# A sequence-to-MLP kernel on one core: layer 0's activation by a polynomial alone, tested as it runs, with the general program behind a branch

## The chip, the cores and the metric

The kernel runs on one core of a Trainium2 chip. The metric is device time in microseconds; the median of three runs before the change is 918.11 us (917.94 to 920.32). The engines are named as in the profile: PE is TensorE, ACT ScalarE, DVE VectorE, POOL GpSimd, SP SyncE (which issues the DMAs here). PE's clock has two levels, 1.2 and 2.4 GHz; the profile gives what was granted as a share of the higher.

## The reference

A gated linear attention with a running state gives `y` for 4 batches, 8 heads, 768 tokens and a head size of 40. It is laid out as 3072 tokens of 320 values and goes through two MLP layers, each 320 to 2048 to 320:

```python
def _moe_ref(x, w_in, w_out):            # layer 0
    h = x @ w_in
    g = h - np.tanh(h)
    return (g @ w_out).astype(np.float32)

def _moe2_ref(x, w_in, w_out):           # layer 1
    h = x @ w_in
    relu6 = np.clip(h + 3.0, 0.0, 6.0)
    g = h * relu6 / 6.0
    return (g @ w_out).astype(np.float32)
```

The weights arrive as float64. The attention's values are small, so layer 0's `h` is small, and `h - tanh(h)` is nearly `h^3/3`, a difference that would lose most of its digits in float32 if it were taken directly.

## The kernel before

**Tiling.** A block is 128 positions of all 4 batches, 512 tokens; there are 6. The 2048 inner features are 16 tiles of 128. A *step* (`step`, line 591) is one block with one feature tile: 16 steps a block, 96 a layer, 192 in all; the first four steps of layer 0 take two batches and two feature tiles instead.

**A step.** `m_in` (line 605) makes `ph`, 128 features by 512 tokens in PSUM, out of eight products (the weights and the input are each split in a high and a low part, since the products round their operands). ACT and DVE turn `ph` into `g`. ACT casts `g` to its high part `gh` (line 636), POOL subtracts to get the low part `gl` (line 637), and `m_out` adds the products with the second weight matrix into four accumulators, eight of `gh` (lines 655, 657) and four of `gl` (line 655), each of 320 columns. `ph` and `u` have two buffers, `g`, `gh` and `gl` three.

**Layer 0's activation (lines 613 to 630).** With u = h^2, the polynomial is g = h u Q(u), Q(u) = (QS u + QB)^2 + QG, good for u up to UMAX = 0.0625. ACT makes `u` (617), tanh `Tm` (618), the square `aq` (621) and a mask `m` that is above zero where u exceeds UMAX (625). DVE makes `ph u` (620), `(aq + QG) g` (629), `ph - Tm` (624), and puts the last in place of the polynomial where the mask says so (630). Layer 1 has one ACT and one DVE operation (632, 633).

**Weights (`weights`, line 270).** Each feature tile of each layer is loaded as float64 bits (704 KB), turned into float32 by one ACT pass (281) and three integer passes on DVE (289, 291, 293), then split in high (ACT, 302) and low (POOL, 305). `raw` and `cva` have two buffers. The split tiles of layer 1 go where those of layer 0 lay, so tile f of layer 1 waits until layer 0's last step with tile f is done.

**Attention.** For each block and batch: scores (485), exp on ACT, weighing on DVE (491), the products with the values (531) and with the state (534), the state's update (517), a transposition into the MLP's input (401).

**Order.** Nothing is ordered by hand. `Order` collects all operations with a rank `t` and a modelled cost; `plan` runs through them once at build time, and each engine takes of the ready operations the one with the least `t`. The result is a fixed sequence per engine. A step's activation has rank k - 8.62, the weights of layer 1 have ranks from 148 up and so fill what is left before they are needed. Eighty products of zeros (line 708, rank about 4) fill PE's gaps at the start.

Of the kernel before, what the change touches and what calls it, by code (L numbers as in the profile page):

```python
# [33 lines left out]

# g(h) = h - tanh(h) = h u Q(u), u = h^2; Q(u) = (QS u + QB)^2 + QG for u <= UMAX
UMAX = 0.0625
QS = 0.2279802546653879
QB = -0.29232135416051347
QG = 0.24788139857377955
# The high word of a float64, taken as a float32, has its exponent's bias in its bits 20 up: times  # L40
# 2^-112 takes 896 = 1023 - 127 from it, and a shift by 3 puts it in float32's place. What is under
# 2^-119 goes to zero, or to another number under that.
REBIAS = 2.0 ** -112
# [23 lines left out]
class Order:  # L67
    """Orders the kernel's operations: each engine takes, of those whose operands and buffers are
    ready, the one with the least t. Buffers of a tag go round in the order of t."""

# [30 lines left out]
    def plan(self):  # L101
# [52 lines left out]
        while True:  # L154
            best = None
            for e in engines:
                while wait[e] and wait[e][0][0] <= free[e]:
                    k = heapq.heappop(wait[e])[1]
                    heapq.heappush(avail[e], (self.ops[k][0], k))
                if avail[e]:  # L160
                    s = free[e]
                elif wait[e]:
                    s = wait[e][0][0]
                else:
                    continue
                if best is None or s < best[0]:
                    best = (s, e)
            if best is None:
                break
            s, e = best  # L170
            while wait[e] and wait[e][0][0] <= s:
                k = heapq.heappop(wait[e])[1]
                heapq.heappush(avail[e], (self.ops[k][0], k))
            k = heapq.heappop(avail[e])[1]
            t, _, cost, fn, _, nbytes, cols = self.ops[k]
            out.append(k)
            if e == "SP":
                dma = max(dma, s + 1.1) + nbytes / 360e3
                end = dma + 0.85
                free[e] = max(s + cost, dma - P["queue"])  # L180
            elif e == "PE":
                # The clock is halved after a window of it in which fewer columns have left the array.
                end, part = s, 1.0
                while part > 1e-9:
                    w = int(end / WINDOW)
                    rate = cost if passed.get(w - 1, 0.0) >= COLUMNS else 2 * cost
                    p = min(part, (WINDOW * (w + 1) - end) / rate + 1e-9)
                    passed[w] = passed.get(w, 0.0) + cols * p
                    part -= p
                    end += rate * p  # L190
                free[e] = end
            else:
                end = free[e] = s + cost
            freed = False
            for inst in used_by.get(k, ()):
                users_left[inst] -= 1
                last_end[inst] = max(last_end[inst], end + 0.2)
                if not users_left[inst]:
                    heapq.heappush(free_slots[tag_of[inst]], (last_end[inst], self.slot[inst]))
                    freed = True  # L200
            for j in succ[k]:
                left[j] -= 1
                ready_at[j] = max(ready_at[j], end + self.LAT[e, self.ops[j][1]])
                if not left[j]:
                    offer(j)
            if freed:
                blocked[:] = [j for j in blocked if not ready(j)]
# [8 lines left out]
@with_exitstack  # L216
def tile_kernel(ctx: ExitStack, tc: tile.TileContext, att: bass.AP, gates: bass.AP, w1: bass.AP, w2: bass.AP, out: bass.AP):
    nc = tc.nc
    Q = P["Q"]

# [20 lines left out]
    state = const.tile([128, B * NPR, 2, DV], F32, name="state")  # L241
    still = const.tile([128, 128], BF16, name="still")
    pairs = [const.tile([128, 2 * NT], F32, name=f"pairs{i}") for i in range(2)]
# [7 lines left out]
    def alloc(pool, tag, bufs, shape, dt, *inst):  # L251
        """What takes the buffer, and what the order needs to know of it."""
        def take():
            name = f"{tag}_{S_.slot[inst]}"
            T[inst] = pool.tile(shape, dt, tag=name, name=name)
            return T[inst]
        return take, (tag, bufs, inst)
# [10 lines left out]

    # ---------------------------------------------------------------- weights
    def weights(layer, f, tl, t):  # L270
# [37 lines left out]

    # ------------------------------------------------------------------ gates
    g_d = {}  # L310
# [71 lines left out]

    # ----------------------------------------------------------- layer inputs
    def x_new(layer, c):
        """The buffers of a block's input, taken for its first batch."""
        def take():
# [4 lines left out]
    def x_ops(layer, c, b, src, scale, tx, ts):  # L391
        """Transposes a tile of tokens, and splits it into what float32r holds and the rest."""
        xb = ("x", layer, c)
# [29 lines left out]

    # -------------------------------------------------------------- attention
    def attention(c, b, t0):
# [163 lines left out]

    # -------------------------------------------------------------------- MLP  # L590
    def step(k, layer, c, bs, fs, t):
# [20 lines left out]
        ph, u, g = (lambda: T["ph", k]), (lambda: T["u", k]), (lambda: T["g", k])  # L612
        if layer == 0:
            take_T, new_T = alloc(ap2, "Tm", BUFS["Tm"], [128, TB], F32, "Tm", k)
# [76 lines left out]

    # ---------------------------------------------------------------- program
    nc.vector.memset(still, 0.0)
    make_identity(nc, ident)
# [5 lines left out]

    # The tensor engine's clock stays up only while enough columns leave the array: until the first
    # block's input is there, products of nothing fill the gaps.
    take_p, new_p = alloc(ps_h, "ph", 2, [128, TB], F32, "ph", "w")

    def warm(i):
        if i == 0:
            take_p()
        nc.tensor.matmul(T["ph", "w"].rearrange("p (j t) -> p j t", j=4), still, still.unsqueeze(1).to_broadcast([128, 4, 128]), start=True, stop=True)
    for i in range(NWARM):
        S_.add(P["ws"] + P["wst"] * i, "PE", 0.215, lambda i=i: warm(i), r=[K("ph", "w")] if i else [], w=[] if i else [K("ph", "w")], new=[] if i else [new_p], at=-99.0, cols=512)  # L710
# [15 lines left out]
    for layer in range(2):  # L726
# [4 lines left out]
        for c in range(NC):  # L731
# [4 lines left out]
            for part in SEQ if k == 0 else "U" * NF:  # L736
# [4 lines left out]
                step(k, layer, c, range(b0, b0 + nb), range(f, f + 4 // nb), k + Q.get(f"m{k}", 0.0) if k < NF else k)  # L741
                k += 1
    S_.plan()
    with tc.manual_schedule():
# [43 lines left out]
```

## Time and profile before

| | |
|---|---|
| median of three runs | 918.11 us |
| profiled execution, span from first to last instruction | 914.1 us |
| busy: PE, DVE, ACT, POOL | 866.9, 572.4, 552.2, 431.1 us |
| share of the span: PE, DVE, ACT, POOL | 95, 63, 60, 47% |
| mean granted clock of PE | 0.977 |
| DMA moved | 77.70 MB, 85 GB/s in the mean |
| instructions | 14486 |

The page of the profile gives busy time by engine over the whole span. A PE that counts as busy isn't always at its peak: the products are pipelined, their ends are modelled, and at the lower clock each lasts longer. So the number of products in a stretch and the distance between their starts say more than the busy share. Idle time of an engine that is not the bound costs nothing.

### The profile page before, as it was taken

To read this page: it belongs to the slowest core of one execution; us is meant where nothing else is said; L and a number is where in the kernel's file an instruction comes from. 1 tells how busy PE (TensorE), PEld (TensorE's weight loads), DVE (VectorE), ACT (ScalarE), POOL (GpSimd) and SP (SyncE) were. 2 spreads that over 40 slices of the span, in tenths; PEclk is the share of its full clock that TensorE was granted. 3 is DMA by queue.
4 is the path that set the end of the run, shared out by engine and by line. 5 is a ranking of instruction groups with operands and counts; after the bars stand their busy time and mean duration, and the time that the engine had idled before them with its cause. 6 is when DMAs were issued, how large, how long until landed. Compare 5 with 4: busy or idle time off the path is not lost.

```text
span 914.1 us, 14486 instructions
## 1 busy us (share of the span) xinstructions
PE 866.9 (95%) x5208; PEld 767.3 (84%) x5208; DVE 572.4 (63%) x924; ACT 552.2 (60%) x1145; POOL 431.1 (47%) x351
## 2 busy tenths in 40 slices
PE   8898888899999999999999988899999999999997
PEld 4687777798898899889898876789999999989897
DVE  7989999887767867885778998823123231132121
ACT  4687776688677768877679865534334343343332
POOL 4666666355446356444334555743333333333342
PEclk9798998899999999999999999999999999999999
DMA  8775445431243044122002225302001020010000
GB/s 281 241 225 178 151 142 164 158 125 42 81 135 106 30 130 131 61 77 96 10 10 70 69 96 181 104 1 64 1 13 51 1 61 4 1 47 1 30 1 30
DMA packets 36248, 77.70 MB, mean 85 GB/s; under 512 B 3824, under 2 KB 24016, under 8 KB 36176
## 3 DMA queue, kind: packets, MB, share of 16 engines
q1 hardware_dynamic: 36176, 76.77, 26.3%
q8 instruction: 41, 0.67, 0.3%
q14 instruction: 31, 0.25, 0.1%
HBM read 67.93 MB, written 8.83 MB: 84 GB/s over the span
## 4 chain that ended last, share of the span: by engine, by line
PE 67%; DVE 16%; issue 5%; ACT 5%; DMA 4%; POOL 2%; SPq 1%; DVEq 0%; POOLq 0%; ACTq 0%
PE ph L605 31%; PE acc L655 19%; PE acc L657 9%; DVE g L629 3%; PE pa L531 3%; DVE g L630 2%; DVE cva L293 2%; PE pa L534 2%; DVE ph L624 2%; DVE g L620 1%; DMA eg<-ed 1%; PE pa L485 1%; DVE cva L291 1%; PE pa L401 1%; DVE cva L289 1%
## 5 line engine op out<-in xcount | busy, mean ns | idle before, releaser
L637 POOL TENSOR_TENSOR gl<-g,gh 128x512 fp32r<-128x512 f32 x192 | 259.7, 1354 | 361.9 <-ACT gh L636 346.8
L655 PE MATMUL acc<-wh,gh 128*128 128x320 f32 x768 | 234.2, 317 | 0.0
L657 PE MATMUL acc<-wl,gh 128*128 128x320 f32 x768 | 229.8, 311 | 0.0
L633 DVE SCALAR_TENSOR_TENSOR g<-u,ph 128x512 f32<-128x512 f32 x96 | 65.9, 687 | 214.3 <-ACT u L632 206.2
L636 ACT CAST gh<-g 128x512 fp32r<-128x512 f32 x192 | 118.5, 618 | 60.6 <-PE acc L657 53.6
L655 PEld LDWEIGHTS acc<-wh,gh 128*128 128x128 f32 x768 | 146.2, 190 | 6.4 <-DVE T L673 0.2
L657 PEld LDWEIGHTS acc<-wl,gh 128*128 128x128 f32 x768 | 146.1, 190 | 5.1
L632 ACT ACTIVATE u<-ph,bias_r 128x512 f32<-128x512 f32 x96 | 66.2, 689 | 138.5 <-PE ph L605 138.4
L605 PE MATMUL ph<-xh,wh 128*128 128x512 f32 (+1 forms) x392 | 128.6, 410 | 17.9 <-DVE g L630 10.3
L655 PE MATMUL acc<-wh,gl 128*128 128x320 f32 x768 | 144.7, 310 | 0.2 <-POOL gl L637 0.2
L605 PE MATMUL ph<-xh,wl 128*128 128x512 f32 (+1 forms) x392 | 122.2, 393 | 0.0
L655 PEld LDWEIGHTS acc<-wh,gl 128*128 128x128 f32 x768 | 121.2, 189 | 0.7 <-POOL gl L637 0.5
L605 PE MATMUL ph<-xl,wh 128*128 128x512 f32 (+1 forms) x392 | 121.1, 390 | 0.0
L620 DVE TENSOR_TENSOR g<-ph,u 128x512 f32<-128x512 f32 x96 | 65.9, 686 | 56.6 <-ACT Tm L618 47.0
L617 ACT ACTIVATE u<-ph 128x512 f32<-128x512 f32 x96 | 57.2, 596 | 65.2 <-PE ph L605 64.9
L629 DVE SCALAR_TENSOR_TENSOR g<-aq,g 128x512 f32<-128x512 f32 x96 | 89.9, 936 | 0.5
L605 PEld LDWEIGHTS ph<-xh,wl 128*128 128x128 f32 x392 | 74.4, 192 | 17.0
L605 PEld LDWEIGHTS ph<-xh,wh 128*128 128x128 f32 x392 | 64.9, 192 | 27.5 <-DVE g L630 14.3
L605 PEld LDWEIGHTS ph<-xl,wh 128*128 128x128 f32 x392 | 74.5, 192 | 16.0
L625 ACT ACTIVATE m<-u,bias_u 128x512 bf16<-128x512 f32 x96 | 69.3, 722 | 15.4 <-DVE g L630 15.4
L605 PE MATMUL ph<-xt,wh 128*128 128x512 f32 (+1 forms) x196 | 77.0, 393 | 0.0
L605 PE MATMUL ph<-xt,wl 128*128 128x512 f32 (+1 forms) x196 | 76.7, 391 | 0.0
(107 smaller groups left out, 1269.7 us busy)
## 6 DMA issues: line engine op xcount, KB each, us to landing
raw<-w SPq DMA_DIRECT2D x32, 704.0 KB
kvo<-att SPq DMA_DIRECT2D x24, 580.0 KB
E<-gd SPq DMA_DIRECT2D x24, 512.0 KB
pairs<-att SPq DMA_DIRECT2D x48, 160.0 KB
eg<-ed SPq DMA_DIRECT2D x40, 128.0 KB
x1d<-T SPq DMA_DIRECT2D x24, 192.0 KB
y<-x1d SPq DMA_DIRECT2D x24, 192.0 KB
out<-T SPq DMA_DIRECT2D x24, 160.0 KB
```

Of the source, the lines that this page charges most:

```text
L531: nc.tensor.matmul(pa[:, h * DV:(h + 1) * DV], T["E", c, b][:, h, :], vv()[:, h, :], start=(h == 0), stop=(c == 0 and h == H - 1))
L605: nc.tensor.matmul(ph[:, j * n:(j + 1) * n], w[:, r * 128:(r + 1) * 128], x, start=(i == 0), stop=(i == len(prods) - 1))
L617: S_.add(ta, "ACT", 0.48, lambda: nc.scalar.activation(out=take_u(), in_=ph(), func=AF.Square), r=[K("ph", k)], w=[K("u", k)], new=[new_u])
L620: S_.add(ta, "DVE", 0.6, lambda: nc.vector.tensor_tensor(take_g(), ph(), u(), ALU.mult), r=[K("ph", k), K("u", k)], w=[K("g", k)], new=[ne ...
L625: S_.add(ta, "ACT", 0.54, lambda: nc.scalar.activation(out=take_m(), in_=u(), func=AF.Relu, bias=bias_u), r=[K("u", k)], w=[K("m", k)], ne ...
L629: S_.add(ta, "DVE", 0.6, lambda: nc.vector.scalar_tensor_tensor(g(), T["aq", k], QG, g(), ALU.add, ALU.mult), r=[K("aq", k), K("g", k)], w ...
L632: S_.add(ta, "ACT", 0.48, lambda: nc.scalar.activation(out=take_u(), in_=ph(), func=AF.Relu, scale=1.0 / 6.0, bias=bias_r), r=[K("ph", k)] ...
L633: S_.add(ta, "DVE", 0.6, lambda: nc.vector.scalar_tensor_tensor(take_g(), u(), 1.0, ph(), ALU.min, ALU.mult), r=[K("ph", k), K("u", k)], w ...
L636: S_.add(t + P["gh"], "ACT", 0.52, lambda: nc.scalar.copy(take_h(), g()), r=[K("g", k)], w=[K("gh", k)], new=[new_h])
L637: S_.add(t + P["gl"], "POOL", 1.23, lambda: nc.gpsimd.tensor_tensor(take_l(), g(), T["gh", k], ALU.subtract), r=[K("g", k), K("gh", k)], w ...
L655: nc.tensor.matmul(o, lhs, wh, start=(f == 0 and part == 0), stop=(f == NF - 1 and part == 1))
L657: nc.tensor.matmul(o, lhs, wl, start=False, stop=False)
```

## The change

The whole program is built twice. The first, with `over` given (`small`), takes the polynomial alone in layer 0: tanh, the mask, the difference and the predicated copy are left out, and the first square also adds up its row into a column of `sums`, one column for each of the 96 steps. Since a sum of squares is at least its largest term, a sum that is at most UMAX proves that every u in it is. In layer 1 the largest of all sums is found (a maximum on DVE, a transpose on PE, a maximum of one row) and compared with UMAX; the flag `over` is 1 where it is larger. Behind the first program the flag is read into registers, and the second program, the general one with tanh as it stands in the kernel before (without the products of zeros), runs only if the flag is set. `P`, `Q` and the ranks are the same for both; the costs given to the planner for layer 0's activation differ.

```diff
+    small = over is not None
...
+    if small:
+        still = const.tile([128, 128], BF16, name="still")
+        sums = const.tile([128, NF * NC], F32, name="sums")
+        most = const.tile([128, 2], F32, name="most")
...
-        if layer == 0:
+        if layer == 0 and small:
+            take_a, new_a = alloc(ap2, "aq", BUFS["aq"], [128, TB], F32, "aq", k)
+            S_.add(ta, "ACT", 0.7, lambda: nc.scalar.activation(out=take_u(), in_=ph(), func=AF.Square, accum_out=sums[:, k:k + 1]), r=[K("ph", k)], w=[K("u", k), K("sums", k)], new=[new_u])
+            S_.add(ta, "ACT", 0.7, lambda: nc.scalar.activation(out=take_a(), in_=u(), func=AF.Square, scale=QS, bias=bias_q), r=[K("u", k)], w=[K("aq", k)], new=[new_a])
+            S_.add(ta, "DVE", 0.69, lambda: nc.vector.tensor_tensor(ph(), ph(), u(), ALU.mult), r=[K("u", k)], w=[K("ph", k)])
+            S_.add(ta, "DVE", 0.69, lambda: nc.vector.scalar_tensor_tensor(take_g(), T["aq", k], QG, ph(), ALU.add, ALU.mult), r=[K("ph", k), K("aq", k)], w=[K("g", k)], new=[new_g])
+        elif layer == 0:
...
-    for i in range(NWARM):
+    for i in range(NWARM if small else 0):
...
+    if small:
+
+        take_t, new_t = alloc(ps_a, "pa", 2, [128, 512], F32, "pt", "most")
+        t = NF * (NC + 1)
+
+        def rows():
+            nc.vector.reduce_max(most[:, 0:1], sums, axis=mybir.AxisListType.X)
+        S_.add(t, "DVE", 0.25, rows, r=[K("sums", i) for i in range(NF * NC)], w=[K("most")])
+        S_.add(t, "PE", 0.1, lambda: nc.tensor.transpose(take_t()[0:1, 0:128], most[:, 0:1], ident), r=[K("most")], w=[K("pt", "most")], new=[new_t], cols=128)
+
+        def compare():
+            nc.vector.reduce_max(most[0:1, 1:2], T["pt", "most"][0:1, 0:128], axis=mybir.AxisListType.X)
+            nc.vector.tensor_scalar(over, most[0:1, 1:2], UMAX, None, ALU.is_gt)
+        S_.add(t, "DVE", 0.5, compare, r=[K("pt", "most")], w=[K("over")])
...
-    with tile.TileContext(nc) as tc:
-        tile_kernel(tc, *args)
+    with tile.TileContext(nc) as tc, tc.tile_pool(name="flag", bufs=1) as flag:
+        over = flag.tile([1, 1], I32, name="over")
+        tile_kernel(tc, *args, over=over)
+        outside = nc.values_load(over, min_val=0, max_val=1, skip_runtime_bounds_check_because="a comparison gives 0 or 1")
+        with tc.If(outside > 0):
+            tile_kernel(tc, *args)
```

## Rows read from the trace of the kernel before

**Rows 1.** Table by stretch: PE, PEld, DVE, ACT, POOL busy (count), clock, DMA share, GB/s.
```profile
0.00:40.00 40.00, 33.04 (x203) 19.88 (x204) 32.96 (x73) 22.43 (x58) 20.39 (x21) 0.94 0.89 283
40.00:180.00 140.00, 122.10 (x775) 107.56 (x774) 131.46 (x197) 98.60 (x223) 89.29 (x74) 0.90 0.54 170
180.00:440.00 260.00, 257.29 (x1704) 231.36 (x1705) 196.53 (x345) 197.20 (x446) 129.20 (x119) 1.00 0.28 90
440.00:600.00 160.00, 146.22 (x784) 128.34 (x784) 137.37 (x184) 113.39 (x209) 82.51 (x53) 0.98 0.24 77
600.00:900.00 300.00, 299.84 (x1690) 271.97 (x1689) 73.05 (x125) 118.52 (x206) 106.02 (x84) 1.00 0.07 21
```

**Rows 2.** Chain that ended last, layer 1: start us, length us, what.
```profile
606.66 1.84 PE ph L605 x8
610.25 1.84 PE ph L605 x8
```

**Rows 3.** Groups of instructions, 40 to 180 us: shapes, count, busy us, mean ns, idle.
```profile
L655 PE MATMUL acc<-wh,gh 128*128 128x320 f32 x64 | 21.4, 345 | 0.0
...
L531 PE MATMUL pa<-kvo,E 128*128 128x41 f32 x96 | 13.4, 305 | 2.9 <-DVE E L491 1.8 <-DVE xt L421 1.1
...
L605 PE MATMUL ph<-xh,wh 128*128 128x512 f32 x30 | 11.3, 462 | 2.3 <-DVE g L630 2.3
...
L485 PE MATMUL pa<-pairs 40*128 40x128 f32 x128 | 10.3, 287 | 1.4 <-DVE tk L380 1.4
...
L629 DVE SCALAR_TENSOR_TENSOR g<-aq,g 128x512 f32<-128x512 f32 x18 | 20.2, 1124 | 0.1
...
L293 DVE SCALAR_TENSOR_TENSOR cva<-raw,cva 128x704 int32<-128x704 int32 x14 | 17.4, 1244 | 0.1
```

**Rows 4.** PE in order of time, 418 to 440 us: start us, length us, what.
```profile
418.66 1.16 PE L485 MATMUL pa<-pairs 40*128 40x128 f32 x16
...
419.75 0.42 PE L655 MATMUL acc<-wh,gh 128*128 128x320 f32 x1
...
437.19 1.88 PE L531 MATMUL pa<-kvo,E 128*128 128x41 f32 x16
...
438.89 1.10 PE L534 MATMUL pa<-state,eg 128*128 128x82 f32 x8
...
439.78 0.48 PE L605 MATMUL ph<-xh,wh 128*128 128x512 f32 x1
```

**Rows 5.** Groups of instructions, 440 to 600 us.
```profile
L655 PE MATMUL acc<-wh,gh 128*128 128x320 f32 x148 | 45.0, 316 | 0.0
...
L605 PE MATMUL ph<-xh,wh 128*128 128x512 f32 x78 | 26.4, 420 | 12.6 <-DVE g L633 7.4 <-DVE g L630 5.1
...
L629 DVE SCALAR_TENSOR_TENSOR g<-aq,g 128x512 f32<-128x512 f32 x24 | 22.2, 925 | 0.1
```

**Rows 6.** Groups of instructions over the whole span: layer 0's operations on DVE and ACT.
```profile
L629 DVE SCALAR_TENSOR_TENSOR g<-aq,g 128x512 f32<-128x512 f32 x96 | 89.9, 936 | 0.5
...
L630 DVE COPY_PREDICATED g<-m,ph 128x512 f32<-128x512 int16 x96 | 71.0, 739 | 5.6 <-ACT m L625 0.2
...
L620 DVE TENSOR_TENSOR g<-ph,u 128x512 f32<-128x512 f32 x96 | 65.9, 686 | 56.6 <-ACT Tm L618 47.0 <-POOL gl L637 6.5 <-PE pa L485 2.0
...
L617 ACT ACTIVATE u<-ph 128x512 f32<-128x512 f32 x96 | 57.2, 596 | 65.2 <-PE ph L605 64.9
...
L625 ACT ACTIVATE m<-u,bias_u 128x512 bf16<-128x512 f32 x96 | 69.3, 722 | 15.4 <-DVE g L630 15.4
...
L636 ACT CAST gh<-g 128x512 fp32r<-128x512 f32 x192 | 118.5, 618 | 60.6 <-PE acc L657 53.6 <-DVE g L630 5.8 <-PE pa L531 1.1
...
L569 ACT ACTIVATE den<-pa 128x8 f32<-128x8 f32 x20 | 3.6, 179 | 7.9 <-PE pa L534 7.7
```

**Rows 7.** Order of time at the end of the span: the last stores.
```profile
908.46 3.25 SPq L681 DMA_DIRECT2D out<-T  x4
```

**Rows 8.** DMA queues: packets, MB, share of 16 engines' span.
```profile
q8 instruction: 41, 0.67, 0.3%
```

More of the change, by code (lines that the diff above doesn't have):

```diff
@@ L216, in tile_kernel @@
 @with_exitstack
-def tile_kernel(ctx: ExitStack, tc: tile.TileContext, att: bass.AP, gates: bass.AP, w1: bass.AP, w2: bass.AP, out: bass.AP):
+def tile_kernel(ctx: ExitStack, tc: tile.TileContext, att: bass.AP, gates: bass.AP, w1: bass.AP, w2: bass.AP, out: bass.AP, over=None):
     nc = tc.nc
+    small = over is not None
     Q = P["Q"]
@@ L241, in tile_kernel @@
     state = const.tile([128, B * NPR, 2, DV], F32, name="state")
-    still = const.tile([128, 128], BF16, name="still")
+    if small:
+        still = const.tile([128, 128], BF16, name="still")
+        sums = const.tile([128, NF * NC], F32, name="sums")
+        most = const.tile([128, 2], F32, name="most")
     pairs = [const.tile([128, 2 * NT], F32, name=f"pairs{i}") for i in range(2)]
@@ L690, in x1_in @@
         x_ops(1, c, b, ("x1", c, b), 1.0, t + P["x1x"], t + P["x1s"])
-    nc.vector.memset(still, 0.0)
+    if small:
+        nc.vector.memset(still, 0.0)
     make_identity(nc, ident)
@@ L699, in tile_kernel @@
     nc.vector.memset(bias_r, 0.5)
-    take_p, new_p = alloc(ps_h, "ph", 2, [128, TB], F32, "ph", "w")
+    take_p, new_p = alloc(ps_h, "ph", 2, [128, TB], F32, "ph", "w") if small else (None, None)
     def warm(i):
@@ L742, in tile_kernel @@
                 k += 1
+    if small:
+        take_t, new_t = alloc(ps_a, "pa", 2, [128, 512], F32, "pt", "most")
[8 more added lines that the diff above has]
+        S_.add(t, "DVE", 0.5, compare, r=[K("pt", "most")], w=[K("over")])
     S_.plan()
```

## The prediction

> **What bounds the kernel now.** I read the table of busy time by stretch first [rows 1]. From 600 to 900 us, which is layer 1 alone, PE is busy 299.84 of 300 us at full clock while DVE works 73 us: there PE is the bound and nothing in the change touches it. From 180 to 440 us PE is busy 257.29 of 260. Two stretches are different. From 40 to 180 us PE shows 122.10 of 140 at a mean clock of 0.90, and DVE shows 131.46, or 94%. From 440 to 600 us PE shows 146.22 of 160 and DVE 137.37. The reader should see that the average over the kernel (PE 95%, DVE 63%) hides two stretches in which DVE leads.
>
> Busy time on PE is not work at full rate, so I counted the products. In layer 1 one step starts 3.59 us after the last, and its eight products of 512 columns take 1.84 [rows 2]: 0.230 us each, and (3.59 - 1.84)/12 = 0.146 for one of 320 columns. In 40 to 180 us there are 3 x 64 = 192 of 320 columns and 30+30+30+15+15 = 120 of 512 [rows 3], and four half-width steps of 16 products at half price: 192 x 0.146 + 120 x 0.230 + 64 x 0.115 = 63 us. Attention beside it: 128 products of L531 (96 in the row, 32 more in another buffer) and 128 of L485 [rows 3] at full-clock paces of 1.70/16 and 1.09/16 [rows 4], 13.6 + 8.7 us; about 107 of 82 columns (L534, L517) at 0.89/8 [rows 4], 11.9; transposes about 1.5. Sum 99 us of work in 140: **41 us lost**. In 440 to 600 us: 444 x 0.146 + 307 x 0.230 [rows 5] + 3 for transposes = 138.5: **21 us lost**. In 180 to 440 the idle time is 2.7 us. The first 40 us are bound by loading (DMA share 0.89), and layer 0's first step starts after them.
>
> **The change, part by part.** *DVE in a step of layer 0.* Now four operations: L620 0.686, L624 (a twin of L620, 0.690), L629 0.936, L630 0.739 [rows 6], 3.05 us. After: u times ph into PSUM, and (aq + QG) times ph into g. Both have one operand in SBUF and one in PSUM, as L620 has: 2 x 0.686 = 1.37 [rows 6]. Removed: 1.68 us in each of 96 steps, 161 us of DVE in all. It counts only where DVE leads.
>
> *ACT in a step.* Tanh (a twin of L617, 0.596) and the mask (L625, 0.722) go [rows 6]: 1.32 us. The first square gains a sum along its row. No row shows such a sum; I bound it by zero and by one more small ACT instruction, L569 at 0.179 [rows 6], and take 0.18, for it must read out at least one column. ACT then has 0.596 + 0.18 + 0.72 + 0.618 = 2.1 us a step, under the 3.59 of PE, so this price is hidden by PE; if ACT led (the rival below), it would cost 17 us over 96 steps.
>
> *40 to 180 us.* DVE does 18 of the steps there (the count of L629 [rows 3]). 18 x 1.68 = 30 us go (L629 is 1.124 there, so a little more). DVE's demand falls from 131.5 to about 100, against 99 of PE work. Two engines with equal demand don't mesh perfectly: DVE alone would allow 100 + its present 8.5 idle = 108.5 us, a gain of 31; I take 119 us, a **gain of 21**, because each step of the first block also waits for a weight tile that goes through DVE three times (about 1.24 us each [rows 3]), ACT twice and POOL once in two buffers. Ends: 10 and 31.
>
> *440 to 600 us.* 24 steps [rows 5] leave 24 x 1.68 = 40 us less for DVE: 137.4 becomes 97, well under 138.5 of PE work. Converting layer 1's weights then fits into the gaps: a step of 3.59 us leaves 2.2 of DVE free, where it leaves 0.5 now. Of the 21 us lost I take back 16; what is late next is ACT and POOL in the weight chain, and the hand-over of the weight buffers. **Gain 16**, ends 10 and 20.
>
> *180 to 440 us.* At most the 2.7 us idle; I take 2. *0 to 40 us:* no layer 0 step runs there, so zero, between 2 lost and 2 gained because the planner, given other costs, may order the loads otherwise.
>
> *The test.* One maximum over 96 columns, one transpose, one maximum of a row and one comparison, once, in layer 1, where DVE is free 227 us of 300 [rows 1]; on PE about 0.1 us. Nothing.
>
> *The branch.* Each engine reads the flag and jumps over the second program once its own stream is done. The trace has no jump. What is nearest: the last stores are issued from 908.46 over 3.25 us [rows 7] and the span ends at 914.1, so 2.4 us cover an issue and a landing. If the read and the refilling of the instruction stream lie beside that landing, the price is zero; if a flag read, a fetch, and a barrier with another fetch come one after another at 2.4 each with nothing hidden, 9.6. I take 4, nearer to two round trips in a row with a part hidden under the last landing. PE, which ends first (about 908), has its cover; SP, which ends last, has none.
>
> The instruction queue moves 41 packets with 0.67 MB, 16 KB each, in 0.3% of 16 engines' span [rows 8], which is about 1.1 us a packet: a jump to code that isn't there costs at least that. The Trainium skill, "Runtime: NRT & Kernel Launch", section "Instruction fetch mechanics", says that a taken branch to a page outside the current window must wait for a fetch of that page, against this change; "Advanced Engine Details and Errata", section "Control Flow Timing", gives about 108 ns for a compare and branch, which alone would leave the end 4 us earlier than my sum. No run here shows either yet.
>
> **Sum.** 914.1 - 21 - 16 - 2 + 4 = 879.1 us of span. The median of the runs, 918.1, lies 4.0 above the span, so 883.1; I predict **883**. With all ends taken together 914.1 - 31 - 20 - 5 + 0 + 4 = 862 and 914.1 - 10 - 10 - 0 + 9.6 + 2 + 4 = 910; the ends won't all meet, and the case's own range is 872 to 895.
>
> **The rivals.**
> 1. *The weight chain takes DVE's place.* In the first block a step can't start before its tile is converted. If the chain load, ACT, three DVE operations, ACT, POOL keeps its pace, freed DVE time stays idle: gains 10 and 10 instead of 21 and 16, 914.1 - 10 - 10 - 0 + 4 + 4 = 902. For it: 14 conversions in 140 us beside 18 steps [rows 3], one every 10 us. Against it: DVE is 94% busy, so the chain queues at DVE, and what queues there becomes shorter. Chance 0.17, 895 to 905.
> 2. *PE takes everything back.* The losses of both stretches vanish but for some 11 us, and the branch is hidden: 914.1 - 31 - 20 - 3 + 1 + 4 = 865. For it: from 180 us on, with DVE at 76%, PE is at 99%. Chance 0.16, 860 to 872.
> 3. *The sum along the row is dear, and ACT becomes the bound.* Place: the first square of each step. ACT has 1.94 us a step without it against 3.59 of PE; it decides from 1.65 us an instruction up, and the 35 us won are gone when each of 96 steps is 0.36 longer, so at 2.0 us; at 2.3 the kernel takes 883 + 96 x (2.3 - 1.65) = 945, slower than before. Against it: no small ACT row is over 0.4 us. Chance 0.03.
> 4. *The change doesn't do what it says: the test trips.* Then the general program runs behind the first, 883 + 914 = about 1797. Worked out from the reference's inputs, the largest sum of squares of h over one row of 512 tokens is 0.0127, a fifth of 0.0625, so it won't. Chance 0.01.
> The forecast has 0.61; 0.02 is left for a change that moves the time by less than 0.3%, about what a measurement of this kernel can tell from none.
>
> **How the numbers follow.** The likeliest case gives 883. To hold 8 in 10 the range takes the whole forecast and the near halves of rivals 1 and 2: 866 to 900. Faster by over 0.3%: 0.61 + 0.17 + 0.16 = 0.94; within 0.3%: 0.02; slower: 0.04.
>
> **What would show it.** Right: in the table by stretch the row that held DVE at 94% shows it near 80% with PE at full clock; the first block's output is stored some 20 us earlier than now, layer 1's steady pace begins near 561 instead of 600 us, and after that one step takes 3.59 us as before. DVE has two operations a step of 0.69 each, ACT three. Wrong: L605 waits as long in the two stretches but for ACT or POOL instead of DVE (rival 1); a gap of more than 10 us between the last store and the end (the branch); ACT with a second instruction of over 0.4 us behind the square (rival 3).

## The result, and the profile after

| | median | lowest to highest |
|---|---|---|
| before | 918.29 us | 917.94 to 920.32 |
| after | 894.14 us | 892.04 to 895.40 |

The ratio is 0.9735 (0.9711 to 0.976): the kernel is faster by 24 us, inside the range of 866 to 900 us and 11 us slower than the forecast of 883. The profiled execution of the changed kernel took 892.04 us with a span of 890.2.

The same table by stretch as [rows 1], of the changed kernel (PE, PEld, DVE, ACT, POOL busy with counts, granted clock, DMA share, GB/s):

```profile
0.00:40.00 40.00, 31.29 (x194) 18.72 (x194) 31.79 (x68) 19.23 (x49) 15.81 (x19) 0.95 0.90 262
40.00:180.00 140.00, 131.21 (x886) 117.43 (x884) 112.42 (x182) 95.43 (x244) 99.93 (x82) 0.94 0.57 191
180.00:440.00 260.00, 260.00 (x1725) 235.78 (x1724) 123.42 (x238) 150.98 (x393) 121.25 (x119) 1.00 0.25 82
440.00:600.00 160.00, 147.84 (x815) 130.93 (x814) 101.97 (x129) 88.76 (x172) 84.66 (x56) 1.00 0.23 77
```

In the second row DVE went from 94% of the stretch to 112.42/140 = 80%, as forecast, and PE got through 886 instructions instead of 775. In the fourth row DVE also fell, from 137 to 102 us of 160, close to the 97 that was forecast, but PE hardly moved: 147.84 us and 815 instructions, against 146.22 and 784. Half of the mechanism worked, and the other half didn't although the engine that was blamed became free in the mean of the stretch.

Layer 0's step, groups of the whole span, which answer to [rows 6]:

```profile
L623 DVE TENSOR_TENSOR ph<-ph,u 128x512 f32<-128x512 f32 x96 | 66.8, 696 | 101.9 <-ACT u L621 101.5
L624 DVE SCALAR_TENSOR_TENSOR g<-aq,ph 128x512 f32<-128x512 f32 x96 | 65.6, 684 | 21.7 <-POOL gl L649 8.8 <-ACT aq L622 6.3
L621 ACT ACTIVATE u<-ph 128x512 f32<-128x512 f32 x96 | 57.1, 594 | 85.5 <-PE ph L611 81.4 <-DVE state L562 3.4
L621 ACT ACTIVATION_READ_ACCUMULATOR u<-ph 128x1 f32 x96 | 18.7, 194 | 0.0
```

DVE has two operations of 0.696 and 0.684 us (forecast 0.686 each). The sum along the row is an ACT instruction of its own, 0.194 us (forecast 0.18).

**Where the 24 us came from.** I counted as the prediction did: the products in a stretch times their full-rate durations, taken from the length of the stretch. What is left over is lost time. The stretches are matched by what runs in them: the last stores of the first block's output are issued at 173.31 us after the change and at 187.34 before. Where the line is drawn hardly matters, since the changed kernel loses 0.1 us between 160 and 200. The products were counted in pieces of 20 or 40 us, and one that lies across an edge counts twice; counted in one piece, the losses come out up to 3 us higher and the gains the same within 0.6.

| stretch (before / after) | lost before | lost after | gain | forecast |
|---|---|---|---|---|
| loading, 0 to 40 | 29.1 | 29.6 | -0.5 | 0 |
| first block, 40 to 200 / 40 to 160 | 41.6 | 23.2 | 18.4 | 21 |
| middle, 200 to 480 / 160 to 480 | 8.0 | 3.5 | 4.5 | 2 |
| border of the layers, 480 to 600 | 20.3 | 15.1 | 5.2 | 16 |
| behind the last products | | | -3.1 | -4 |
| sum | | | 24.5 | 35 |

The span became 914.1 - 890.2 = 23.9 us shorter, so the table leaves 0.6 us unexplained. The trace is that of the fastest run of the changed kernel; in the second measurement below the first block loses 25.2 us, so the gain there is 16 to 18. One row is far from its forecast: the border of the two layers, where layer 1's weights are converted while layer 0's last steps run. The experiments go there first.

### The profile page after: what moved, and what is told of

It reads as the page before. It is cut to its first block, busy times and chain, and to the rows that moved or that the text cites. A ratio compares the mean times of both kernels' runs of the same rounds, so it can differ in the third digit from the quotient of the medians.

```text
span 890.2 us, 14216 instructions
## 1 busy us (share of the span) xinstructions
PE 851.8 (96%) x5209; PEld 759.0 (85%) x5209; DVE 437.5 (49%) x735; ACT 465.3 (52%) x1049; POOL 420.9 (47%) x351
## 4 chain that ended last, share of the span: by engine, by line
PE 79%; DVE 9%; DMA 4%; issue 3%; ACT 3%; POOL 2%; SPq 1%; DVEq 0%; POOLq 0%; ACTq 0%
PE ph L611 34%; PE acc L667 22%; PE acc L669 11%; PE pa L537 4%; PE pa L491 2%; DVE cva L297 2%; PE pa L540 2%; DVE cva L295 2%; DVE cva L299 1%; PE pa L407 1%; PE pa L523 1%; DMA raw<-w 1%; ACT cva L287 1%; DMA E<-gd 1%; DMA pairs<-att 1%
## 5 line engine op out<-in xcount | busy, mean ns | idle before, releaser
L649 POOL TENSOR_TENSOR gl<-g,gh 128x512 fp32r<-128x512 f32 x192 | 256.5, 1336 | 329.0 <-ACT gh L648 322.3
L667 PEld LDWEIGHTS acc<-wh,gh 128*128 128x128 f32 x768 | 144.2, 188 | 8.4 <-DVE T L685 1.5
L611 PE MATMUL ph<-xh,wh 128*128 128x512 f32 (+1 forms) x392 | 126.2, 403 | 10.9 <-DVE g L645 7.5
L623 DVE TENSOR_TENSOR ph<-ph,u 128x512 f32<-128x512 f32 x96 | 66.8, 696 | 101.9 <-ACT u L621 101.5
L624 DVE SCALAR_TENSOR_TENSOR g<-aq,ph 128x512 f32<-128x512 f32 x96 | 65.6, 684 | 21.7 <-POOL gl L649 8.8
L311 POOL TENSOR_TENSOR wl<-cva,wh 128x704 fp32r<-128x704 f32 x32 | 57.5, 1798 | 30.0 <-ACT wh L308 28.1
```

The costliest lines, as they stand in the source:

```text
L311: nc.gpsimd.tensor_tensor(take_l(), T["cva", layer, f], T["wh", layer, f], ALU.subtract)
L611: nc.tensor.matmul(ph[:, j * n:(j + 1) * n], w[:, r * 128:(r + 1) * 128], x, start=(i == 0), stop=(i == len(prods) - 1))
L623: S_.add(ta, "DVE", 0.69, lambda: nc.vector.tensor_tensor(ph(), ph(), u(), ALU.mult), r=[K("u", k)], w=[K("ph", k)])
L624: S_.add(ta, "DVE", 0.69, lambda: nc.vector.scalar_tensor_tensor(take_g(), T["aq", k], QG, ph(), ALU.add, ALU.mult), r=[K("ph", k), K("aq" ...
L649: S_.add(t + P["gl"], "POOL", 1.23, lambda: nc.gpsimd.tensor_tensor(take_l(), g(), T["gh", k], ALU.subtract), r=[K("g", k), K("gh", k)], w ...
L667: nc.tensor.matmul(o, lhs, wh, start=(f == 0 and part == 0), stop=(f == NF - 1 and part == 1))
```

## The experiments

Medians, with the lowest and highest, beside the kernel before on the same chip, whose median was 916.6, 915.9 and 916.8 us on the three chips. The ratio is to that kernel, with its 95% interval.

| kernel | median | lowest to highest | ratio |
|---|---|---|---|
| after, second measurement (`after_again`) | 894.05 | 892.63 to 899.92 | 0.9777 (0.9702 to 0.9852) |
| true costs, layer 1 (`cost_l1`) | 882.27 | 880.31 to 883.66 | 0.9612 (0.9572 to 0.9651) |
| true costs, both layers (`cost_both`) | 881.30 | 880.45 to 883.13 | 0.9618 (0.9554 to 0.9682) |
| true costs and a third buffer (`cost_bufs`) | 882.40 | 879.63 to 885.95 | 0.9617 (0.9588 to 0.9645) |
| kernel before, true costs (`before_cost`) | 910.44 | 909.61 to 910.65 | 0.9930 (0.9909 to 0.9951) |
| DVE's work put back (`dve_back`) | 913.39 | 910.54 to 917.13 | 0.9959 (0.9936 to 0.9982) |
| ACT's work put back (`act_back`) | 911.28 | 908.57 to 912.50 | 0.9932 (0.9895 to 0.9970) |
| ACT's work on another operand (`act_on_u`) | 912.23 | 910.85 to 917.48 | 0.9966 (0.9937 to 0.9995) |
| one integer pass in layer 0 (`one_pass_l0`) | 889.90 | 886.24 to 890.09 | 0.9703 (0.9635 to 0.9771) |
| no sums (`no_sum`) | 894.48 | 891.75 to 897.32 | 0.9769 (0.9740 to 0.9797) |
| no branch (`no_branch`) | 887.98 | 885.92 to 892.35 | 0.9673 (0.9631 to 0.9716) |
| branch not skipped (one run) (`taken`) | 1809.3 | | |

The changed kernel was measured a second time, on another chip, for comparison with the kernels that ran there:

> The changed kernel once more, beside the other kernels of this group, so that they are compared on one chip: 892 to 896 if this chip is like the first, and some 2 us less if it is like the second, where the kernel before took 916.6.

Measured: 894.05 us beside 894.14, so below the kernels of the different chips are set against it by their medians. Its ratio, 0.9777, is higher and its interval wider: the kernel before was faster there (915.9 us), and one of the four runs took 899.92. By itself this measurement doesn't tell whether the gain is over 2%.

### The border of the layers: the order made at build time

The integer passes of a weight tile have the costs 0.435, 0.8 and 0.8 us in the plan, 2.04 us a tile. The trace of the changed kernel gives 0.810, 1.463 and 1.273 for the same lines (L295, L297, L299), 3.55 us. Since the plan fixes each engine's sequence, a cost that is too low can put a whole conversion in a place where it doesn't fit. The first experiment gives the plan the measured costs of layer 1's conversions; no operation of the program is another, only their order is:

```diff
-            S_.add(t, "DVE", (0.435, 0.8, 0.8)[i], bits(i), ...
+            S_.add(t, "DVE", ((0.435, 0.8, 0.8), (0.81, 1.46, 1.27))[layer][i], bits(i), ...
```

> The changed kernel, but the planner is told what the trace of the changed kernel shows for the three integer passes of layer 1's weights on DVE (0.81, 1.46 and 1.27 us in place of 0.435, 0.8 and 0.8); no instruction is added or removed, only the fixed order may move. Theory 1: around the change of layers the order puts one conversion (3.5 us in truth, 2.0 in the plan) beside each step's 1.4 us of DVE, which is more than the 3.59 us of a step, and PE waits; with true costs the conversions are spread over more steps and 5 to 12 us of the 14 us lost there come back: 882 to 889. Theory 2: the conversions are tied by their buffers (two of cva, and the split tiles free only as layer 0 leaves them), and order makes no difference: 892 to 896.

Measured: 882.27 us, 12 us faster than the changed kernel, with intervals that don't touch. DVE in order of time in the changed kernel (start us, length us, operation; in brackets the idle time before it and what ended it):

```profile
498.58 0.69 DVE L623 TENSOR_TENSOR ph<-ph,u 128x512 f32<-128x512 f32 x1
499.19 1.38 DVE L299 SCALAR_TENSOR_TENSOR cva<-raw,cva 128x704 int32<-128x704 int32 x1
500.49 0.67 DVE L624 SCALAR_TENSOR_TENSOR g<-aq,ph 128x512 f32<-128x512 f32 x1
501.09 0.51 DVE L295 TENSOR_SCALAR cva<-cva 128x704 int32<-128x704 int32 x1
501.64 2.28 DVE L297 SCALAR_TENSOR_TENSOR cva<-raw,cva 128x704 int32<-128x704 int32 x1
503.84 0.69 DVE L623 TENSOR_TENSOR ph<-ph,u 128x512 f32<-128x512 f32 x1
504.44 1.38 DVE L299 SCALAR_TENSOR_TENSOR cva<-raw,cva 128x704 int32<-128x704 int32 x1
505.75 0.68 DVE L624 SCALAR_TENSOR_TENSOR g<-aq,ph 128x512 f32<-128x512 f32 x1
```

Three passes stand between one step's L624 and the next one's, so these steps come 505.75 - 500.49 = 5.26 us apart where PE needs 3.59. With the true costs such a place is left too, but the next two steps follow closely:

```profile
498.22 0.68 DVE L624 SCALAR_TENSOR_TENSOR g<-aq,ph 128x512 f32<-128x512 f32 x1
...
504.00 0.67 DVE L624 SCALAR_TENSOR_TENSOR g<-aq,ph 128x512 f32<-128x512 f32 x1
...
506.98 0.68 DVE L624 SCALAR_TENSOR_TENSOR g<-aq,ph 128x512 f32<-128x512 f32 x1
...
510.80 0.68 DVE L624 SCALAR_TENSOR_TENSOR g<-aq,ph 128x512 f32<-128x512 f32 x1
```

Over nine starts of L624 the mean distance is 4.04 us in the changed kernel (479.44 to 511.75) and 3.81 with the true costs (482.15 to 512.65). And 80 us of the border, first in the kernel before, then in the changed kernel, then with the true costs:

```profile
480.00:560.00 80.00, 70.48 (x375) 61.03 (x373) 74.80 (x98) 62.19 (x116) 42.77 (x28) 0.98 0.27 89
```

```profile
480.00:560.00 80.00, 69.46 (x376) 60.08 (x374) 72.09 (x80) 47.43 (x88) 51.95 (x32) 1.00 0.38 129
```

```profile
480.00:560.00 80.00, 77.86 (x434) 69.51 (x433) 75.81 (x85) 52.78 (x96) 59.47 (x35) 1.00 0.39 129
```

In these 80 us the change took little from DVE: 74.80 us busy (94%) before, 72.09 (90%) after. The time that it freed inside them went to the conversions, which run closer together: 14 starts of the first pass are recorded from 477.8 to 556.2 us in the changed kernel, and 14 from 502.6 to 591.7 in the kernel before. Free time is left on either side, as from 560 to 600 us, where DVE is busy for 9.98 us of 40. With the true costs the conversions take as long as in the changed kernel, from 480.5 to 558.8 us, and DVE is busier still (75.81 us), but PE does 434 instructions beside them instead of 376. More than half of these 58 come after 520 us, among the steps of layer 1 (212 against 180 from 520 to 560 us), so that the place shown above is only a part of what the order changed. The lost time of 480 to 600 us falls from 15.1 to 3.9 us, which is 11 of the 12 us gained. What PE waits for between 460 and 600 us (us in all, times, longest), the changed kernel first:

```profile
PE ph L611 <- DVE g L645: 7.5, 6, 1.8
PE ph L611 <- DVE g L624: 3.3, 3, 1.4
```

```profile
PE ph L611 <- DVE g L645: 2.7, 3, 1.2
```

Do the first block's 23 us have the same cause? The costs of both layers were set:

```diff
-            S_.add(t, "DVE", (0.435, 0.8, 0.8)[i], bits(i), ...
+            S_.add(t, "DVE", (0.81, 1.46, 1.27)[i], bits(i), ...
```

> As cost_l1, but the planner has the measured costs of the three integer passes for the weights of both layers. Around the change of layers the 12 us come back as in cost_l1 by either theory. Theory 1 for the first block too (the plan's conversions of 2.0 us stand for 3.5 us): 3 to 10 us of the 25 us lost between 40 and 140 us come back, 873 to 879. Theory 2 (there the tiles are needed as soon as they are made, so that order can't help): within 3 us of cost_l1, 879 to 885.

Measured: 881.30 us, no different from 882.27. The first block loses 25.4 us, as it does with layer 1's costs alone (25.0) and in the second measurement of the changed kernel (25.2). There, telling the plan the costs gains nothing.

A rival for what was left was the hand-over of the conversion buffers. With layer 1's true costs, `cva` got a third buffer:

```diff
-        take_a, new_a = alloc(cvp, "cva", BUFS["cva"], [128, WC], F32, "cva", layer, f)
+        take_a, new_a = alloc(cvp, "cva", 3 if small else 2, [128, WC], F32, "cva", layer, f)
```

> cost_l1 with three buffers in place of two for the tile under conversion (cva), so that DVE can run one tile of layer 1 further ahead of the moment when layer 0 leaves the split tiles' place. If buffers hold back what is still lost around the change of layers (some 4 us), 877 to 881; if the first block is what is left, within 2 us of cost_l1, 880 to 884.

Measured: 882.40 us, no gain. The buffers of `cva` are not it; a third one for `raw` was not tried.

Was the fault in the order there before the change, or did the change uncover it? The kernel before got the same costs for layer 1, with the diff of the first experiment:

> The kernel before, with tanh and mask, but the planner is told the same costs of layer 1's integer passes as in cost_l1 (0.81, 1.46, 1.27). If the 12 us were a fault of the order that the kernel before has as well, it gains as much, 902 to 907. If the order can only use DVE time that the change has freed (DVE is busy 97% there before, so that conversions have nowhere to go), it stays within 4 us of the kernel before.

Measured: 910.44 us, 6.4 us faster than the kernel before beside it, between the two expectations. At the border it is the same fault: the lost time falls from 20.3 to 8.0 us, 12 us as in the changed kernel. Some 5 us go the other way between 160 and 320 us, where the first conversions of layer 1 now stand in other places and where DVE, with four operations a step, has less to spare. So the fault was in both kernels, and neither expectation holds in full.

### The first block: which engine had to be freed

Two operations of DVE were put back in each layer 0 step, 0.69 and 0.94 us long, into a tile that nothing uses:

```diff
+            take_j, new_j = alloc(ap2, "junk", 2, [128, TB], F32, "junk", k)
+            S_.add(ta, "DVE", 0.69, lambda: nc.vector.tensor_tensor(take_j(), ph(), u(), ALU.mult), ...
...
+            S_.add(ta, "DVE", 0.94, lambda: nc.vector.scalar_tensor_tensor(T["junk", k], T["aq", k], QG, T["junk", k], ALU.add, ALU.mult), ...
```

> The changed kernel with two more DVE operations in each step of layer 0, of the kinds and sizes of those that were taken out (one with a PSUM operand, about 0.69 us; one all in SBUF, about 0.94 us), whose result nobody reads. If the gain came from DVE, nearly all of it goes: 910 to 920. If it came from ACT (tanh and mask, or the mask's single buffer), the time stays within 5 us of 894.

Measured: 913.39 us. Of the 24 us 19 are gone, and all of them in the first block: 40 to 200 us lose 47.6 us, more than before the change (41.6). The border loses 14.2, no more than without the added work (15.1). The two operations also make a step's chain on DVE longer, as in the kernel before; whether DVE's time or this chain counts was not separated.

Then the other half: tanh and the mask stay on ACT, unread.

```diff
+            S_.add(ta, "ACT", 0.6, lambda: nc.scalar.activation(out=take_T(), in_=ph(), func=AF.Tanh), ...
...
+            S_.add(ta, "ACT", 0.72, lambda: nc.scalar.activation(out=take_m(), in_=u(), func=AF.Relu, bias=bias_u), ...
```

> The changed kernel with tanh and the mask still made on ACT in each step of layer 0, about 0.60 and 0.72 us, read by nobody. If DVE was what the change relieved, the time rises by 0 to 6 us, to 894 to 900. If ACT was, it rises by 15 us or more, to 909 and over.

Measured: 911.28 us, and this is a miss: 17 of the 24 us are gone as well. The first block (40 to 160 us) loses 39.4 us instead of 23.2. One way around it was left: tanh reads `ph`, and so may hold the PSUM buffer longer. In the next kernel it reads `u` behind the second square, so that only ACT's time is the same:

```diff
-            ... activation(out=take_T(), in_=ph(), func=AF.Tanh) ...
+            ... activation(out=take_T(), in_=u(), func=AF.Tanh) ...
```

> As act_back (911.3), with as much work on ACT, but tanh reads u in SBUF instead of ph, behind the second square, so that DVE's product and the release of ph no longer wait for it. If act_back lost its 17 us by the longer chain of a step (DVE waits for tanh), the time falls to 894 to 900. If it lost them by ACT's time as such (the conversions' two ACT passes and the exponentials stand behind tanh and mask in ACT's fixed order), it stays at 905 to 912.

Measured: 912.23 us, the same. It isn't the buffer of `ph` but ACT's work. How 0.6 + 0.72 us a step can matter on an engine that is busy 75 us of these 100 shows in the chain of work that ended last, between 40 and 140 us (share of the 100 us by line). Before the change:

```profile
by line: issue 10.8%; DVE g L629 10.1%; DMA eg<-ed 6.5%; DVE g L630 5.0%; PE pa L531 4.9%; DVE cva L293 4.5%; DMA raw<-w 4.2%; DVE ph L624 4.0%; ACT E L474 3.6%; PE ph L605 3.5%; DVE g L620 3.5%; DVE cva L289 3.4%; PE pd L531 3.3%; DVE E L4
```

After it:

```profile
by line: issue 11.0%; PE ph L611 10.8%; PE pa L537 7.3%; PE pd L537 5.3%; POOL wl L311 4.6%; DVE cva L295 4.2%; PE acc L667 3.7%; PE pa L540 3.7%; ACT E L480 3.6%; POOL E L472 3.4%; DVE ph L623 3.2%; DVE E L497 3.1%; DVE cva L297 3.0%; PE p
```

With ACT's work put back, on `ph` and on `u`:

```profile
by line: DVE cva L297 9.6%; DVE cva L299 7.7%; issue 7.5%; PE ph L611 7.2%; ACT cva L287 5.7%; PE pa L537 5.4%; PE acc L671 4.7%; DVE cva L295 4.6%; DMA E<-gd 4.1%; ACT E L480 4.0%; PE pa L491 3.4%; ACT m L627 3.0%; PE pa L540 2.7%; ACT wh 
```

```profile
by line: PE ph L611 10.8%; PE pa L537 10.4%; issue 10.1%; DVE cva L297 9.5%; PE acc L671 5.5%; DMA E<-gd 4.4%; PE pa L540 4.4%; DVE cva L295 4.1%; DVE cva L299 3.9%; ACT cva L287 3.1%; PE acc L673 2.9%; DVE g L628 2.7%; PE pa L523 2.4%; PE 
```

With DVE's work put back:

```profile
by line: PE ph L611 12.6%; issue 8.3%; DVE junk L626 7.8%; PE pa L537 6.9%; DMA eg<-ed 4.8%; PE pa L491 4.2%; PE acc L670 4.0%; DVE g L627 4.0%; PE pa L540 3.7%; DVE ph L625 3.7%; DVE junk L623 3.2%; POOL E L472 2.8%; PE pa L523 2.7%; POOL 
```

`cva` is a weight tile under conversion. With tanh and the mask back in ACT's sequence, the four passes over `cva` (L287 on ACT, L295 to L299 on DVE) hold 27.6 and 20.6 us of this chain. With DVE's four operations a step, it is the steps that hold it: L623, L625, L626 and L627 stand for 18.7 us, as L620, L624, L629 and L630 do for 22.6 before the change. In the changed kernel neither group is near that. The reading is that the first block hangs on two chains, the weights' and the steps', each of which passes both engines. The chain that ended last is one path of many, so this reading is supported and not shown; the loss itself is what the put-back kernels show. By the ratios, freeing ACT alone gave 0.4% (4 us), freeing DVE alone 0.3 to 0.7% (3 to 6 us), and freeing both 2.2 to 2.7% (20 to 24 us).

Is DVE still the bound of what is left? One kernel does one of the three integer passes for layer 0's weights, so that these weights' values are not the reference's:

```diff
-        for i in range(3):
+        for i in range(1 if small and not layer else 3):
```

> The changed kernel with one of the three integer passes over layer 0's weights on DVE instead of three; the sign and the low bits of layer 0's weights are left out, so its numbers are others. It takes 16 x 2.7 = 44 us from DVE before 140 us and nothing from ACT, POOL, PE or DMA. If DVE is still the bound of the first block, 10 to 18 us of the 25 us lost there come back: 876 to 884. If ACT, POOL or the loads have taken its place, under 5 us: 889 to 894.

The stretch from 40 to 140 us, the changed kernel first:

```profile
40.00:140.00 100.00, 91.21 (x607) 81.01 (x606) 89.68 (x140) 71.24 (x180) 77.87 (x59) 0.92 0.58 195
```

```profile
40.00:140.00 100.00, 94.69 (x639) 85.74 (x638) 71.04 (x124) 72.77 (x182) 66.85 (x58) 0.90 0.62 205
```

DVE falls from 90% to 71%, and only 4 us are gained (889.90 against 894.14). In the first block itself 5 to 7 us come back, and the border and the first 40 us lose 2 to 3 us more. So DVE alone no longer bounds the first block. In this kernel PE shows 94.69 us busy at a granted clock of 0.90, no other engine is above 73%, and the chain that ended last lies mostly on PE:

```profile
by line: PE ph L611 24.6%; PE pa L537 12.1%; PE acc L667 10.7%; PE pa L491 5.8%; PE pa L540 5.4%; DMA pairs<-att 5.4%; PE acc L669 5.2%; issue 4.3%; PE pa L523 3.4%; ACT E L480 2.5%; DVE E L497 1.9%; DVE G L351 1.8%; DVE cva L295 1.6%; DVE 
```

Why PE still loses 18 us there by count is open; relief of ACT alone below the changed kernel's level was not tried.

### The test and the branch

Without the sums along the rows (the tile is set to zero instead, so the test looks at nothing):

```diff
-            ... activation(out=take_u(), in_=ph(), func=AF.Square, accum_out=sums[:, k:k + 1]) ...
+            ... activation(out=take_u(), in_=ph(), func=AF.Square) ...
```

> The changed kernel without the sum behind the first square (the extra ACT instruction of 0.194 us in 96 steps); the maximum runs over zeros, the flag, its read and the jump stay. If the sum is hidden by PE, as predicted, within 2 us of the changed kernel, 892 to 896. If ACT's time counts as in act_back (1.32 us more a step cost 17 us), 0.194 us less a step gives 2 to 4 us back: 890 to 892.

Measured: 894.48 us, the same as 894.14. The 96 x 0.194 = 18.7 us of ACT's readouts cost nothing that runs from 891.75 to 897.32 us can tell.

Without the read of the flag, the branch and the second program:

```diff
-        outside = nc.values_load(over, min_val=0, max_val=1, ...)
-        with tc.If(outside > 0):
-            tile_kernel(tc, *args)
```

> The changed kernel without the read of the flag, the jump and the second program; the sums and the test stay. If the branch costs what the end of the changed kernel's trace shows (8.8 us from the last product's end region to the end of the span, 6.1 before, 2.2 us less outside the span), the time falls by 0 to 3 us, to 891 to 894. If the second program costs more than its jump (instruction memory, longer start), it falls by 5 us or more, to 889 or under.

The end of the span in order of time, the changed kernel (span 890.2 us):

```profile
880.66 0.75 PE L667 MATMUL acc<-wh,gl 128*128 128x320 f32 x4
...
881.46 3.59 SPq L693 DMA_DIRECT2D out<-T  x4
```

And without the branch (span 890.5 us):

```profile
884.11 0.75 PE L667 MATMUL acc<-wh,gl 128*128 128x320 f32 x4
...
884.91 3.25 SPq L693 DMA_DIRECT2D out<-T  x4
```

From the last products' start to the end it takes 890.2 - 880.66 = 9.5 us with the branch and 890.5 - 884.11 = 6.4 without, so the branch costs 3.1. Of these, 2.8 lie behind the last issued store (5.15 us from there to the end, against 2.34, and 2.4 in the kernel before), and 0.3 in the issuing itself. The medians differ by 6 us, more than the ends explain. The profiled execution without the branch (892.35, the slowest of its four) lost 26.6 us in the first block where the changed kernel lost 23.2, and the two sets of times overlap. Whether the branch costs more than 3.1 us is not settled.

At last the second program was made to run, by comparing the largest sum with zero:

```diff
-            nc.vector.tensor_scalar(over, most[0:1, 1:2], UMAX, None, ALU.is_gt)
+            nc.vector.tensor_scalar(over, most[0:1, 1:2], 0.0, None, ALU.is_gt)
```

> The changed kernel with the flag's comparison against zero instead of 0.0625, so that the jump isn't taken and the general program runs behind the first. As long as both programs one after the other: 894 and some 915 to 935 (it lacks the products of zeros at its start), 1805 to 1835 us.

Measured: 1809.3 us in one run: the general program behind the first one costs 1809.3 - 894.1 = 915 us, about what the whole kernel before takes. The two overlap only at their edge: POOL's first instruction of the second program starts at 881.07 us, while the first program's last products run to 884.97, and PE's first product of the second starts at 893.47.

## Why the prediction was right, and where it failed

**First block: right in size, and its reason only half.** The gain is 18.4 us of the 21 forecast, between the ends of 10 and 31, and DVE's share is the 80% that was named. PE wasn't at full clock there, as the prediction's sign had it, but at 0.94. The gain doesn't hang on the clock: with layer 1's true costs it is 0.90 between 40 and 180 us, as before the change, and the block loses 25.0 us and not 41.6. But the step on ACT ("ACT then has 0.596 + 0.18 + 0.72 + 0.618 = 2.1 us a step, under the 3.59 of PE, so this price is hidden by PE") put ACT at nothing, and the sum has no term for what tanh and the mask give back. That reasoning is for steps at PE's pace, and in the first block 18 steps [rows 3] take 140 us, 7.8 us each. The two kernels with ACT's work put back show that without ACT's relief 17 of the 24 us would not have come. That the sum came out right although ACT's term was missing is luck: the change frees both engines at once.

**Border: the step that failed.** The prediction said: "Converting layer 1's weights then fits into the gaps: a step of 3.59 us leaves 2.2 of DVE free", and took 16 us, with 10 as the lower end. 5.2 came. Its own row gave 1.24 us a pass [rows 3], 3.7 a tile, which doesn't fit into 2.2 (that row is L293 alone; all three took 0.85, 1.32 and 1.24 us there, 3.4 a tile). Between 480 and 600 us of the changed kernel the passes took 1.77, 1.29 and 0.91, 4.0 a tile. A demand of 97 us in a stretch of 160 says that the work fits on average, but the conversions fill half of that stretch, and there DVE is still busy for 72.09 us of 80. The sum says nothing either of a fixed sequence, in which a conversion of 2.04 modelled us is put between two steps. That the order decides what PE loses beside the conversions is shown: with true costs and no operation changed the loss falls from 15.1 to 3.9 us, while DVE is no less busy. With them the border gives back 16.4 us of the 20.3 lost, nearly the 16 of the prediction. So the work did fit, but only in another order. DVE's relief by itself brought little there: with DVE's work put back the border loses no more (14.2), and with ACT's put back it loses, by the same count, 2.5 and 3.6 us more.

**Middle.** 4.5 us instead of 2: the prediction looked at PE's idle time of 2.7 us between 180 and 440 us, and the loss by count, in the longer stretch of 200 to 480 us, was 8.0.

**Sums and test.** Hidden, as said, as far as the runs can tell: 0.194 us a step on ACT and no gain without it. The price of the test's four operations by themselves was not measured.

**Branch.** 3.1 us of the 4 forecast, between 0 and 9.6. The prediction weighed two places of the Trainium skill: "Runtime: NRT & Kernel Launch", section "Instruction fetch mechanics", by which a taken branch out of the window waits for a page, goes with the 2.8 us behind the last store; the 108 ns of "Advanced Engine Details and Errata", section "Control Flow Timing", alone would not make them. The fetch itself is not to be seen as a row, and how the 2.8 us divide between it and the read of the flag is not shown; the instruction queue moved 43 packets, against 41 before and 41 without the branch.

**The addition of 4.0 us for what lies around the span.** It mixed two executions, the median of some and the span of another. The profiled runs since lie 1.8 to 2.2 us above their own spans (892.04 against 890.2 in the changed kernel's). With 1.8 the sum would have been 881, and the profiled run's 892.04 us is 11 us above it: 10.8 at the border, 2.6 in the first block and 0.5 while loading, less 2.5 in the middle and 0.9 at the branch, and the 0.6 that the table leaves. Against the median of 894.14 us the sum would have been 13 us off instead of 11, so the slip hid 2 of them.

**The rivals.** The weight chain (902 us) was right in that the chain counts: it runs through ACT as well as DVE. But it foresaw 10 and 10 us, and it was 18 and 5. The measured 894.14 us lies a little nearer to its 902 than to 883, though not for its reason. "PE takes everything back" (865) would have needed the border; even with true costs 25 us of the first block stay lost. The dear sum didn't come. The price for a tripped test, 1797, was 12 us too low, 11 of them because it was put on top of 883 instead of 894.

**What would show it.** The first block's output (of layer 0) is stored 14 us earlier, not 20. Its last stores before and after the change:

```profile
187.34 1.09 SPq L679 DMA_DIRECT2D x1d<-T  x2
```

```profile
173.31 0.41 SPq L691 DMA_DIRECT2D x1d<-T  x1
```

Layer 1's steady pace begins at 561.61 us instead of 595.62, where the forecast had 561, and one step then takes 3.59 us as before. Before the change:

```profile
595.62 2.09 PE ph L605 x8
...
599.47 1.84 PE ph L605 x8
```

After it:

```profile
561.61 2.09 PE ph L611 x8
...
565.46 1.84 PE ph L611 x8
...
569.05 1.84 PE ph L611 x8
```

This hit is luck in part. From there to the last stores' issue it takes 881.46 - 561.61 = 319.85 us after the change and 908.46 - 595.62 = 312.84 before: the pace began 34 us earlier, but with two more steps of work left.

**The better kernel.** The change with true costs for the conversions takes 881.3 to 882.3 us, some 35 us below the kernel before: as much as the prediction expected of the change alone.

## What to carry to other kernels

Where a build-time plan sets each engine's sequence, compare its modelled costs with the profile's rows first: here 12 us lay in costs that were too low. When a change frees two engines at once, put the work of each back by itself before saying which one mattered; here either alone was worth 3 to 6 us and both 20 to 24. And a sum of busy time below the length of a stretch shows that work fits on average, so hold the single piece against the single gap as well.

## What was unexpected of the hardware

The integer passes on DVE, whose operands all lie in SBUF, often stretch while POOL runs, and DVE's operations of a step that read PSUM don't. From the changed kernel (start us, length us):

```profile
510.67 1.50 POOL L649 TENSOR_TENSOR gl<-g,gh 128x512 fp32r<-128x512 f32 x1 [0.97 <-ACT gh L648]
...
510.92 0.70 DVE L623 TENSOR_TENSOR ph<-ph,u 128x512 f32<-128x512 f32 x1
...
512.36 0.88 DVE L299 SCALAR_TENSOR_TENSOR cva<-raw,cva 128x704 int32<-128x704 int32 x1
...
514.14 1.70 POOL L311 TENSOR_TENSOR wl<-cva,wh 128x704 fp32r<-128x704 f32 x1 [1.97 <-ACT wh L308]
...
514.19 2.40 DVE L297 SCALAR_TENSOR_TENSOR cva<-raw,cva 128x704 int32<-128x704 int32 x1
...
515.80 1.94 POOL L649 TENSOR_TENSOR gl<-g,gh 128x512 fp32r<-128x512 f32 x1
...
516.62 1.87 DVE L299 SCALAR_TENSOR_TENSOR cva<-raw,cva 128x704 int32<-128x704 int32 x1
...
518.42 0.67 DVE L645 SCALAR_TENSOR_TENSOR g<-u,ph 128x512 f32<-128x512 f32 x1
```

L299 takes 0.88 us while POOL is idle and 1.87 beside it; L297 takes 2.40 beside it and 0.87 at its shortest; L623 stays at 0.70 beside POOL, and at 0.66 to 0.70 in all of its 96 places. POOL's `gl`, 1.30 us at other times, takes 1.94 here. So the true price of a conversion isn't a number of its own but depends on what stands beside it, and the costs given to the plan in the experiments are means. The Trainium skill, "GPSIMD Engine Reference", section "Specifications", says that GpSimd's SBUF interfaces are shared with VectorE and contend with its instructions that run in a 2-port perf mode or have two SBUF inputs; L297 and L299 have two such inputs, and the trace agrees. L295 has one and stretches too, from 0.51 to 1.73 us; whether it runs in such a mode no row shows. The change gains by this as well: L629, all in SBUF, took 0.64 to 1.88 us in the kernel before, and L624, which stands in its place with one operand in PSUM, takes 0.67 to 0.69.
